# Rounded 512-column matmuls whose moving columns lie and are read in pieces of eight

## The chip, the cores and the metric

The kernel runs on one core of one Trainium2 chip. The metric is the device time of one execution in microseconds (us); lower is better.

## The reference

Linear attention with random features, followed by a layer norm and a two-layer FFN with a residual. There are 8 batches, 8 heads, 576 positions, 64 columns per head and 128 features; the model width is 512 and the FFN's inner width 2048. All data are float32.

```python
def phi(x):                                   # x: q or k, scaled by 64 ** -0.25
    h = x @ omega.T - sum(x * x) / 2
    return exp(h - max(h)) / sqrt(128)

kv  = einsum('bhsm,bhsd->bhmd', phi(k), v)
num = einsum('bhsm,bhmd->bhsd', phi(q), kv)
den = einsum('bhsm,bhm->bhs', phi(q), phi(k).sum(over s)) + 1e-6
x   = num / den                               # 4608 rows of 512 columns
xn  = (x - mean(x)) / sqrt(var(x) + 1e-6) * g_ln
out = x + relu(xn @ w_ch1) @ w_ch2
```

## The kernel before

One Python planner (`Plan`) writes the program. Pieces of work are generators that name the engine and an assumed cost for each step; the planner picks, step by step, which piece goes next on which engine, and so fixes each engine's instruction order before the program is built. The costs are constants in the code, so the order does not depend on what a step really takes on the chip.

The 4608 rows of x are cut into 9 blocks of 512 rows (index `t`), each of 4 chunks of 128 rows (`i`). Attention work for later blocks is woven between the FFN matmuls of earlier ones.

**Rounded matmuls.** The FFN matmuls work on float32 numbers split in two parts of type fp32r: a rounded copy, and the rest (the number minus the rounded copy, rounded again). A product of two such numbers takes three matmuls: high x high, low x high, high x low. `w[:, 0]`, `xnT[:, 0]` and `hl[:, 0]` are high parts, `[:, 1]` the low ones. Every such matmul has a stationary operand of 128 x 128 (loaded by an LDWEIGHTS of its own, PEld in the profile) and a moving operand of 128 x 512, and writes one PSUM bank of 512 columns.

- `mm1(t, f)` (lines 798 to 800): for each of the 16 slices `f` of the inner width, 4 steps over the model width by 3 matmuls. Stationary are columns of `w_ch1`, moving is `xnT` (the 512 rows of the block as columns). `relu` (lines 809, 811) turns the bank into `hl`.
- `mm2(t, f)` (lines 831 to 833): for each slice `f` and each chunk `i`, 3 matmuls. Stationary are 128 columns of `hl`, moving is a row block of `w_ch2`. Sums are kept in four banks over all `f`; `result` (line 842) adds x and stores.
- `gen_q2` (lines 589, 590): the projection of q for the later blocks, two rounded matmuls per 512 columns, with `qs` as the moving operand: `qs` holds the rounded q in partitions 0 to 63 and the rest of it in 64 to 127.

**Where the moving operands come from.** `xnT` is filled in `gen_xnT1` from four transposes in one PSUM bank: line 775 (ScalarE) copies and rounds, line 777 (VectorE) subtracts to get the rest. `xnT` has one buffer, so the block's four chunks are transposed between the last `mm1` of one block and the first of the next, under the last `mm2`. `w_ch2` comes as 64-bit numbers whose two words `gen_w` puts together on ScalarE and VectorE (lines 352 to 385), element by element, for the 16 slices of each weight once, mostly in the first 150 us. `qs` is loaded from `qD` and rounded in lines 580 and 582, element by element too.

**Other matmuls** that the text speaks of: line 308 is a bf16 matmul of 128 x 256 columns on constant data, which keeps TensorE busy before the first FFN matmul; lines 483, 514, 554 and 681 are attention matmuls on unrounded float32 with 64 rows or 64 columns of the array; line 771 holds the transposes.

In all, 6 x 576 FFN matmuls and 2 x 56 for q are rounded with 512 columns.

Of the kernel before, what the change touches and what calls it, by code (L numbers as in the profile page):

```python
# [17 lines left out]
ALU = mybir.AluOpType  # L18
# [4 lines left out]
P = 128  # L23
B, H, S, D = 8, 8, 576, 64
M = 128
DM = H * D
DFF = 4 * DM
NP = H // 2
NK = DM // P
NF = DFF // P  # L30
# [9 lines left out]
QB = 256  # L40
NB = N // QB
# [27 lines left out]
class Plan:  # L69
# [73 lines left out]
    def free(self, *names):  # L143
        for n in names:
            assert n not in self.places, n
            self.places[n] = self.cur.seen()
            self.cur.holds -= n[0] == "b" and 0 < self.cur.holds
            self.wake(lambda w: w[0] == "get" and n in w[1])

    def done(self, key):  # L150
        self.made[key] = self.cur.seen()
        self.wake(lambda w: w == ("wait", key))
# [38 lines left out]
def favor_ffn(ctx, tc, kT, kTr, vF, vR, qT, qD, omT, gT, w1, w2, out):  # L191
# [12 lines left out]
    nc = tc.nc  # L204
# [8 lines left out]
    def f32(ap):  # L213
        return ap.bitcast(F32)

    def act(n, k=1, c=0.09):
        return "run", {ACT: k * (c + 0.00084 * n)}

    def dve(n, k=1, c=0.065):
        return "run", {DVE: k * (c + 0.00105 * n)}  # L220

    def us(eng, t):
        return "run", {eng: t}

    def dma(n):
        return "run", {SP: n * 4e-6 / 0.36}
# [13 lines left out]
    def wait(*key):  # L240
        return "wait", key
# [4 lines left out]
    def tile_of(tag, shape, dtype=F32, pool=None):  # L246
        pool = pool or (wp if tag[1].isdigit() and tag[0] == "w" else small if tag[0:2] in ("kv", "mb", "st") or tag[0] == "v" else sb)
        return pool.tile(shape, dtype, tag=tag, name=tag, bufs=1)

    def heads_of(tag):  # L250

        n = H * (D + 1)
        return tile_of(tag, [P, -(-n // LINE) * LINE])[:, 0:n].rearrange("p (a b) -> p a b", b=D + 1)

    def bank(tag, n=512):
        return tile_of(tag, [P, 512], F32, ps)[:, 0:n]
# [12 lines left out]
    def at_now():  # L269
        return b_at if mlp_on else banks  # L270
# [22 lines left out]
    om_raw = tile_of("hid0", [P, M])  # L293
    if TILED:
        om = const.tile([P, M], F32, name="om")
        om_hi = const.tile([P, M], F32R, name="om_hi")
        om_lo = const.tile([P, M], F32R, name="om_lo")
# [12 lines left out]
    def gen_const():  # L310
        yield dma(P * M)
        nc.sync.dma_start(om_raw, omT)
        yield dve(M)
        if TILED:
            nc.vector.tensor_scalar(out=om, in0=om_raw, scalar1=SC, scalar2=None, op0=ALU.mult)
# [11 lines left out]
    def slot(h):  # L327
        return (h % 2) * 4 + h // 2 if TILED else h

# [62 lines left out]
    kvs, phis, xs, xnTs, pvs, pvt = {}, {}, {}, {}, {}, {}  # L392
# [30 lines left out]
    def gen_k(b, c, kraw, v, early, t_v, n_kp):  # L423
# [14 lines left out]
        def values():  # L438
            yield us(DVE, 0.08)
            nc.vector.memset(v[:, :, D : D + 1], 1.0)  # L440
            done(("v", b, c))
# [64 lines left out]
        plan.add(rank, values())  # L506
        if TILED:
            t_b = yield "get", at_now(), 2
# [28 lines left out]
    def gen_q(blk, j):  # L537
# [8 lines left out]

        if TILED:
            t_b = yield "get", at_now(), 2
# [20 lines left out]
    def gen_q2(blk, j, s):  # L569
        rank = plan.cur.rank  # L570
        q_turn = yield "get", turn["q"]
        t_q = yield "get", n_big
        qraw = tile_of(t_q, [P, 2 * QB])
        yield dma(P * 2 * QB)
        nc.sync.dma_start(qraw, qD[blk, j, s].rearrange("p a b -> p (a b)"))
        yield wait("om2")
        t_s = yield "get", n_big
        qs = tile_of(t_s, [P, 2 * QB], F32R)
        yield act(2 * QB)
        nc.scalar.copy(out=qs, in_=qraw)  # L580
        yield us(DVE, 0.85)
        nc.vector.tensor_tensor(out=qs[D:P], in0=qraw[D:P], in1=f32(qs[D:P]), op=ALU.subtract)  # L582
        free(t_q, q_turn)
        t_b = yield "get", at_now()

        plan.cur.after = max(plan.cur.after, plan.cur.end + LATE)
        yield us(PE, 0.46)
        pq = bank(t_b)
        nc.tensor.matmul(pq, om_hi, qs, start=True, stop=False)  # L589
        nc.tensor.matmul(pq, om_lo, qs, start=False, stop=True)  # L590
        free(t_s)
        yield from features(blk, j, s, t_b, pq)

# [7 lines left out]
    def features(blk, j, s, t_b, pq):  # L601
        t_c = yield "get", n_big
        qc = tile_of(t_c, [P, 2 * QB])
        eng = yield "run", {ACT: 0.48, DVE: 0.62} if blk >= T // QB else {ACT: 0.58}
        copy(eng, qc, pq)
        free(t_b)
        mx_turn = yield "get", turn["mx"]
        t_m = yield "get", n_big
        mx = tile_of(t_m, [P, 2 * QB])
        yield us(POOL, 1.9)  # L610
        nc.gpsimd.partition_all_reduce(mx, qc, P, bass_isa.ReduceOp.max)  # L611
        done(("mx", blk, j, s))
        yield us(DVE, 0.95 if blk >= T // QB else 0.6)
        nc.vector.tensor_tensor(out=qc, in0=qc, in1=mx, op=ALU.subtract)  # L614
        free(t_m, mx_turn)
        yield act(2 * QB)
        nc.scalar.activation(out=qc, in_=qc, func=AF.Exp)  # L617
        phis[blk, j, s] = t_c, qc.rearrange("p (a b) -> p a b", b=QB)
        done(("phi", blk, j, s))

    def phi(blk, h, cols):
        p, o = h // 2, h % 2
        s, i = (o, p % 2) if TILED else (p % 2, o)
        return phis[blk, p // 2, s][1][:, i, cols]
# [137 lines left out]
            plan.add(plan.cur.rank, gen_xnT1(t, i, xn, t_n, xn_turn))  # L762

    def gen_xnT1(t, i, xn, t_n, xn_turn):
        xnT = xnTs[t][1]
        yield wait("ident")
        t_b = yield "get", at_now()
        yield us(PE, 0.46)
        pt = bank(t_b).rearrange("p (a b) -> p a b", b=P)
        for k in range(NK):  # L770
            nc.tensor.transpose(pt[:, k], xn[:, k * P : (k + 1) * P], ident)  # L771
        free(t_n, xn_turn)
        cols = slice(i * P, (i + 1) * P)
        yield us(ACT, 0.5)
        nc.scalar.copy(out=xnT[:, 0, :, cols], in_=pt)
        yield dve(DM)
        nc.vector.tensor_tensor(out=xnT[:, 1, :, cols], in0=pt, in1=f32(xnT[:, 0, :, cols]), op=ALU.subtract)  # L777
        free(t_b)
        done(("xnT", t, i))


    hid = {}

    def mm1(t, f):
        for k in range(NK):
            yield wait("w", 1, f // NK * NK + k)
        for i in range(TC):
            yield wait("xnT", t, i)
        if not mlp_on:
            mlp_on.append(True)  # L790
        t_x, xnT = xnTs[t]
        t_b = yield "get", b_h
        ph = bank(t_b)
        for k in range(NK):
            yield us(PE, 3 * 0.225)
            w = wparts[1, f // NK * NK + k]
            cs = slice(f % NK * P, (f % NK + 1) * P)
            nc.tensor.matmul(ph, w[:, 0, cs], xnT[:, 0, k], start=(k == 0), stop=False)  # L798
            nc.tensor.matmul(ph, w[:, 1, cs], xnT[:, 0, k], start=False, stop=False)  # L799
            nc.tensor.matmul(ph, w[:, 0, cs], xnT[:, 1, k], start=False, stop=(k == NK - 1))  # L800
        if f == NF - 1:
            free(t_x)
        plan.add(MOST_URGENT, relu(t, f, t_b, ph))

    def relu(t, f, t_b, ph):
        t_h = yield "get", n_hid
        hl = tile_of(t_h, [P, 2, T], F32R)
        yield act(T, 1, 0.05)
        nc.scalar.activation(out=hl[:, 0], in_=ph, func=AF.Relu)  # L809
        yield dve(T)  # L810
        nc.vector.scalar_tensor_tensor(  # L811
            out=hl[:, 1], in0=ph, scalar=0.0, in1=f32(hl[:, 0]), op0=ALU.max, op1=ALU.subtract
        )
        free(t_b)
        hid[t, f] = t_h, hl
        done(("hid", t, f))

    accs = {}

    def mm2(t, f):  # L820
        yield wait("w", 2, f)
        yield wait("hid", t, f)
        t_h, hl = hid[t, f]
        w = wparts[2, f]
        for i in range(TC):
            if f == 0:
                t_b = yield "get", (b_acc[i],)
                accs[i] = bank(t_b)
            yield us(PE, 3 * 0.225)
            cs = slice(i * P, (i + 1) * P)  # L830
            nc.tensor.matmul(accs[i], hl[:, 0, cs], w[:, 0], start=(f == 0), stop=False)  # L831
            nc.tensor.matmul(accs[i], hl[:, 0, cs], w[:, 1], start=False, stop=False)  # L832
            nc.tensor.matmul(accs[i], hl[:, 1, cs], w[:, 0], start=False, stop=(f == NF - 1))  # L833
            if f == NF - 1:
                plan.add(MOST_URGENT, result(t, i, accs[i]))
        free(t_h)
# [55 lines left out]


TILED = True
LINE = 16
FIRST = 4
N_BIG = 14
# [4 lines left out]
WARM, COLD = 0.0, 5.0  # L902
RW, RS = -10, 1.0
RK, RQ = -36, -28


# [37 lines left out]
```

## Time and profile before

| | |
|---|---|
| median of 3 runs | 1012.5 us (1011.98 to 1012.75) |
| the profiled execution, its own time | 1012.24 us |
| its span from the first to the last instruction | 1010.4 us |
| TensorE busy | 1004.0 us (99%), 6794 matmuls |
| weight loads (PEld) busy | 813.7 us (81%) |
| VectorE busy | 499.9 us (49%) |
| ScalarE busy | 343.1 us (34%) |
| GpSimd busy | 137.1 us (14%) |
| mean granted TensorE clock | 0.999 |

The profile is of one execution. Its page lists, for each engine, the busy time, then groups of equal instructions: line of the program, engine, operation, output tile <- input tiles, shapes and count, and after the bar the busy us, the mean ns of one, and the idle time of the engine just before them with what ended it. A timeline row is: start in us, duration in us, engine, line, operation, and how many are merged into the row (x3). Matmuls are pipelined: the record of one reaches past the start of the next, so what a row of equal matmuls costs is read from their starts and not from their durations. PEld is TensorE's weight load, which runs beside the matmul before it.

### The profile page before, as it was taken

Reading aid. Unit: us, or ns where it says so; the run is one execution under the profiler, and the core shown is the slowest. Engines: PE = TensorE matmul, PEld = TensorE weight load, DVE = VectorE, ACT = ScalarE, POOL = GpSimd, SP = SyncE. Lnnn points to the kernel's source line nnn. Section 1 sums busy time; section 2 is a strip of 40 time slices with the busy share of each in tenths; the row PEclk is TensorE's granted clock in tenths of the full one; section 3 lists DMA queues with packets and bytes.
Section 4 is the critical chain, followed back from the end, with each engine's and each line's share of the span. In section 5 each row is a group of like instructions: output and inputs, shape, how many; then the busy total and the mean of one; then the engine's idle time right before and its main releaser. Section 6 shows DMA issues by size and latency. Waiting matters only on the chain.

```text
span 1010.4 us, 16487 instructions
## 1 busy us (share of the span) xinstructions
PE 1004.0 (99%) x6794; PEld 813.7 (81%) x6794; DVE 499.9 (49%) x1054; ACT 343.1 (34%) x785; POOL 137.1 (14%) x80
## 2 busy tenths in 40 slices
PE   9999999999999999999999999999999999999998
PEld 7877787787778778887888778888888888888886
DVE  6999997375347531673157423751384143113112
ACT  6687755235334520353125321331142011011110
POOL 5000632023001300140005000220031000000000
PEclk9999999999999999999999999999999999999999
DMA  9544332221132100320031100300120010001001
GB/s 353 205 145 162 121 105 73 75 74 64 43 116 76 41 12 1 128 84 1 1 126 64 43 1 11 116 1 1 42 84 1 1 42 1 0 1 42 1 1 42
DMA packets 29740, 63.16 MB, mean 63 GB/s; under 512 B 3424, under 2 KB 3552, under 8 KB 29664
## 3 DMA queue, kind: packets, MB, share of 16 engines
q1 hardware_dynamic: 29664, 62.09, 17.7%
q8 instruction: 54, 0.88, 0.3%
q14 instruction: 22, 0.18, 0.1%
HBM read 52.64 MB, written 9.44 MB: 61 GB/s over the span
## 4 chain that ended last, share of the span: by engine, by line
PE 94%; DVE 4%; DMA 1%; issue 0%; SPq 0%; ACT 0%; DVEq 0%
PE b L798 14%; PE b L831 14%; PE b L800 13%; PE b L799 13%; PE b L832 13%; PE b L833 13%; PE b L681 3%; PE b L514 3%; PE b L483 3%; PE b L771 1%; PE b L589 1%; PE b L590 1%; DMA w<-w 1%; DMA w<-vF 1%; PE b L554 0%; DVE x L842 0%
## 5 line engine op out<-in xcount | busy, mean ns | idle before, releaser
L811 DVE SCALAR_TENSOR_TENSOR hid<-b,hid 128x512 fp32r<-128x512 f32 x144 | 99.4, 690 | 381.2 <-ACT hid L809 381.0
L809 ACT ACTIVATE hid<-b 128x512 fp32r<-128x512 f32 x144 | 86.7, 602 | 457.2 <-PE b L800 456.5
L831 PE MATMUL b<-w,hid 128*128 128x512 f32 x576 | 232.0, 403 | 0.0
L798 PE MATMUL b<-xnT,w 128*128 128x512 f32 x576 | 230.2, 400 | 0.0
L833 PE MATMUL b<-w,hid 128*128 128x512 f32 x576 | 224.8, 390 | 0.0
L832 PE MATMUL b<-w,hid 128*128 128x512 f32 x576 | 224.8, 390 | 0.0
L800 PE MATMUL b<-xnT,w 128*128 128x512 f32 x576 | 224.6, 390 | 0.1
L799 PE MATMUL b<-xnT,w 128*128 128x512 f32 x576 | 224.6, 390 | 0.0
L611 POOL PARTITION_ALL_REDUCE wide<-wide x72 | 136.0, 1927 | 630.4 <-ACT wide L230 463.4
L798 PEld LDWEIGHTS b<-xnT,w 128*128 128x128 f32 x576 | 108.1, 188 | 25.6 <-issue 0.7
L831 PEld LDWEIGHTS b<-w,hid 128*128 128x128 f32 x576 | 108.1, 188 | 25.3 <-issue 0.7
L800 PEld LDWEIGHTS b<-xnT,w 128*128 128x128 f32 x576 | 108.1, 188 | 23.6 <-DVE xnT L777 0.5
L833 PEld LDWEIGHTS b<-w,hid 128*128 128x128 f32 x576 | 108.1, 188 | 23.2
L799 PEld LDWEIGHTS b<-xnT,w 128*128 128x128 f32 x576 | 108.2, 188 | 20.8
L832 PEld LDWEIGHTS b<-w,hid 128*128 128x128 f32 x576 | 108.3, 188 | 20.2
L451 ACT ACTIVATE kp<-b,mb 128x128 f32<-128x128 f32 x272 | 74.7, 388 | 60.9 <-DVE mb L445 60.7
L614 DVE TENSOR_TENSOR wide<-wide,wide 128x512 f32<-128x512 f32 x72 | 63.7, 890 | 10.0 <-POOL wide L611 9.4
L445 DVE TENSOR_REDUCE mb<-b 128x4 f32<-128x512 f32 x72 | 46.6, 683 | 35.5 <-PE b L514 35.5
L617 ACT ACTIVATE wide<-wide 128x512 f32<-128x512 f32 x72 | 45.3, 634 | 45.8 <-DVE wide L614 45.3
L681 PEld LDWEIGHTS b<-kv,wide 128*64 128x64 f32 (+1 forms) x1088 | 40.5, 140 | 11.4 <-issue 8.8
L582 DVE TENSOR_TENSOR wide<-wide,wide 64x512 fp32r<-64x512 f32 x56 | 43.7, 787 | 8.7 <-ACT wide L580 7.2
L230 ACT COPY wide<-b 128x512 f32<-128x512 f32 x60 | 34.1, 593 | 36.0 <-PE b L590 31.2
(70 smaller groups left out, 784.1 us busy)
## 6 DMA issues: line engine op xcount, KB each, us to landing
w<-w SPq DMA_DIRECT2D x32, 512.0 KB, 7.8
wide<-qD SPq DMA_DIRECT2D x56, 256.0 KB, 2.7
out<-x SPq DMA_DIRECT2D x36, 256.0 KB, 2.0
v<-vF SPq DMA_DIRECT2D x28, 260.0 KB, 3.1
wide<-kT SPq DMA_DIRECT2D x28, 256.0 KB, 3.1
wide<-qT SPq DMA_DIRECT2D x8, 256.0 KB, 3.9
w<-vF SPq DMA_DIRECT2D x4, 260.0 KB, 4.8
v<-vR SPq DMA_DIRECT2D x4, 260.0 KB, 4.0
```

Of the source, the lines that this page charges most:

```text
L451: nc.scalar.activation(out=kp[:, j], in_=pk[:, i], func=AF.Exp, scale=1.0, bias=mb[:, j : j + 1])
L611: nc.gpsimd.partition_all_reduce(mx, qc, P, bass_isa.ReduceOp.max)
L614: nc.vector.tensor_tensor(out=qc, in0=qc, in1=mx, op=ALU.subtract)
L681: nc.tensor.matmul(pn[a:z, i], phi(blk, h, slice(cols + a, cols + z)), kvs[b][1][:, h], start=True, stop=True)
L798: nc.tensor.matmul(ph, w[:, 0, cs], xnT[:, 0, k], start=(k == 0), stop=False)
L799: nc.tensor.matmul(ph, w[:, 1, cs], xnT[:, 0, k], start=False, stop=False)
L800: nc.tensor.matmul(ph, w[:, 0, cs], xnT[:, 1, k], start=False, stop=(k == NK - 1))
L809: nc.scalar.activation(out=hl[:, 0], in_=ph, func=AF.Relu)
L811: nc.vector.scalar_tensor_tensor(out=hl[:, 1], in0=ph, scalar=0.0, in1=f32(hl[:, 0]), op0=ALU.max, op1=ALU.subtract)
L831: nc.tensor.matmul(accs[i], hl[:, 0, cs], w[:, 0], start=(f == 0), stop=False)
L832: nc.tensor.matmul(accs[i], hl[:, 0, cs], w[:, 1], start=False, stop=False)
L833: nc.tensor.matmul(accs[i], hl[:, 1, cs], w[:, 0], start=False, stop=(f == NF - 1))
```

## The change

The 512 moving columns of a rounded matmul are taken as 4 groups of 16 pieces of 8 columns: column `c * 128 + a * 8 + b` with `c` below 4, `a` below 16, `b` below 8. Before, column n lay at element n of its row. Now it lies at element `a * 32 + c * 8 + b`. A matmul reads its columns in the old logical order, so that it takes the first eight elements of each 32 across the row, then the second eight, and so on: four passes over 2048 bytes. Its output columns are written in order, side by side, as before. Everything that fills a moving operand puts it into the new layout: `xnT` by the copies out of PSUM, where chunk `i` is group `c`; `w_ch2` and `qD` by the host, which reorders the arrays before the launch (`spread`). Stationary operands (`w_ch1`, `hl`, `om_hi`, `om_lo`) lie as before. `rounded` stands for the 8 former matmul calls; its line number is 786 in the changed kernel. The planner's costs and ranks stay, and the order of the instructions on every engine is the same as before.

```diff
+    def rounded(out, lhsT, rhs, start, stop):
+        nc.tensor.matmul(
+            out.rearrange("p (c a b) -> p c a b", a=AW, b=BW), lhsT,
+            rhs.rearrange("p (a c b) -> p c a b", a=AW, b=BW), start=start, stop=stop,
+        )
...
 def gen_q2(blk, j, s):
-        nc.sync.dma_start(qraw, qD[blk, j, s].rearrange("p a b -> p (a b)"))
+        nc.sync.dma_start(qraw, qD[blk, j, s])
...
-        nc.tensor.matmul(pq, om_hi, qs, start=True, stop=False)
-        nc.tensor.matmul(pq, om_lo, qs, start=False, stop=True)
+        rounded(pq, om_hi, qs, start=True, stop=False)
+        rounded(pq, om_lo, qs, start=False, stop=True)
...
 def gen_xnT1(t, i, xn, t_n, xn_turn):
-        xnT = xnTs[t][1]
+        xnT = xnTs[t][1].rearrange("p h k (a c b) -> p h k a c b", a=AW, b=BW)[:, :, :, :, i]
...
-        cols = slice(i * P, (i + 1) * P)
+        pt = pt.rearrange("p k (a b) -> p k a b", b=BW)
-        nc.scalar.copy(out=xnT[:, 0, :, cols], in_=pt)
+        nc.scalar.copy(out=xnT[:, 0], in_=pt)
-        nc.vector.tensor_tensor(out=xnT[:, 1, :, cols], in0=pt, in1=f32(xnT[:, 0, :, cols]), op=ALU.subtract)
+        nc.vector.tensor_tensor(out=xnT[:, 1], in0=pt, in1=f32(xnT[:, 0]), op=ALU.subtract)
...
 def mm1(t, f):
-            nc.tensor.matmul(ph, w[:, 0, cs], xnT[:, 0, k], start=(k == 0), stop=False)
-            nc.tensor.matmul(ph, w[:, 1, cs], xnT[:, 0, k], start=False, stop=False)
-            nc.tensor.matmul(ph, w[:, 0, cs], xnT[:, 1, k], start=False, stop=(k == NK - 1))
+            rounded(ph, w[:, 0, cs], xnT[:, 0, k], start=(k == 0), stop=False)
+            rounded(ph, w[:, 1, cs], xnT[:, 0, k], start=False, stop=False)
+            rounded(ph, w[:, 0, cs], xnT[:, 1, k], start=False, stop=(k == NK - 1))
...
 def mm2(t, f):                                # the three calls likewise, on accs[i], hl and w
+AW, BW = 16, 8
+def spread(x):
+    x = x.reshape(*x.shape[:-1], -1, AW, BW)
+    return np.ascontiguousarray(np.moveaxis(x, -3, -2)).reshape(*x.shape[:-3], -1)
...
-    qD = np.ascontiguousarray(np.concatenate([q6, q6], axis=3))
+    qD = spread(np.concatenate([q6, q6], axis=3).reshape(NB, 2, 2, P, 2 * QB))
-    w2 = np.ascontiguousarray(moe_w_ch2.reshape(NF, P, DM)).view(np.int64)
+    w2 = spread(moe_w_ch2.reshape(NF, P, DM)).view(np.int64)
```

More of the change, by code (lines that the diff above doesn't have):

```diff
@@ L830, in mm2 @@
             cs = slice(i * P, (i + 1) * P)
-            nc.tensor.matmul(accs[i], hl[:, 0, cs], w[:, 0], start=(f == 0), stop=False)
-            nc.tensor.matmul(accs[i], hl[:, 0, cs], w[:, 1], start=False, stop=False)
-            nc.tensor.matmul(accs[i], hl[:, 1, cs], w[:, 0], start=False, stop=(f == NF - 1))
+            rounded(accs[i], hl[:, 0, cs], w[:, 0], start=(f == 0), stop=False)
+            rounded(accs[i], hl[:, 0, cs], w[:, 1], start=False, stop=False)
+            rounded(accs[i], hl[:, 1, cs], w[:, 0], start=False, stop=(f == NF - 1))
             if f == NF - 1:
```

## The prediction

> **What bounds the kernel now.** I read the page's first part and its clock line, then the chain, then the groups, then single matmuls in time order.
>
> ```profile
> PE 1004.0 (99%) x6794; PEld 813.7 (81%) x6794; DVE 499.9 (49%) x1054; ACT 343.1 (34%) x785; POOL 137.1 (14%) x80
> ...
> PEclk9999999999999999999999999999999999999999
> ...
> PE 94%; DVE 4%; DMA 1%; issue 0%; SPq 0%; ACT 0%; DVEq 0%
> PE b L798 14%; PE b L831 14%; PE b L800 13%; PE b L799 13%; PE b L832 13%; PE b L833 13%; PE b L681 3%; PE b L514 3%; PE b L483 3%; PE b L771 1%; PE b L589 1%; PE b L590 1%; DMA w<-w 1%; DMA w<-vF 1%; PE b L554 0%; DVE x L842 0%
> ```
>
> TensorE is busy for 99% of the span at the full granted clock, and the chain lies on it for 94%. Six lines, 798 to 800 and 831 to 833, hold about 80% of the span. They are the three-part products of the two FFN matmuls; with lines 589 and 590 they are exactly the matmuls that the change touches.
>
> ```profile
> L831 PE MATMUL b<-w,hid 128*128 128x512 f32 x576 | 232.0, 403 | 0.0
> L798 PE MATMUL b<-xnT,w 128*128 128x512 f32 x576 | 230.2, 400 | 0.0
> L833 PE MATMUL b<-w,hid 128*128 128x512 f32 x576 | 224.8, 390 | 0.0
> L832 PE MATMUL b<-w,hid 128*128 128x512 f32 x576 | 224.8, 390 | 0.0
> L800 PE MATMUL b<-xnT,w 128*128 128x512 f32 x576 | 224.6, 390 | 0.1
> L799 PE MATMUL b<-xnT,w 128*128 128x512 f32 x576 | 224.6, 390 | 0.0
> ...
> L589 PE MATMUL b<-wide,om_hi 128*128 128x512 f32 x56 | 21.8, 389 | 0.0
> L590 PE MATMUL b<-wide,om_lo 128*128 128x512 f32 x56 | 21.8, 389 | 0.0
> ```
>
> That is 6 x 576 + 2 x 56 = 3568 rounded matmuls, and TensorE sat idle before none of them for more than 0.1 us in sum. The 390 ns of a record is not what one costs, since they overlap; that is the step from one start to the next. A long quiet stretch near the end gives it (timeline; first and last of 182 rounded matmuls in a row):
>
> ```profile
> 959.83 0.39 PE L832 MATMUL b<-w,hid 128*128 128x512 f32 x1
> ...
> 1000.86 0.39 PE L800 MATMUL b<-xnT,w 128*128 128x512 f32 x1
> ```
>
> 41.03 us over 181 steps is 226.7 ns each. 3568 x 226.7 ns = 809 us: one price, paid 3568 times, is four fifths of the kernel. So the question is only what the new way of reading the moving columns does to this step.
>
> **What the step is made of.** The nearest other matmul at full clock with a weight load before each is the bf16 warming matmul of 256 columns, 36 of them in a row:
>
> ```profile
> 38.07 0.27 PE L308 MATMUL b<-spin 128*128 128x256 bf16 x1
> ...
> 38.58 4.09 PE L308 MATMUL b<-spin 128*128 128x256 bf16 x36
> ```
>
> (4.09 - 0.27) / 35 = 109.1 ns for 256 columns, 218.3 ns for 512, though that holds two starts. The rounded step is 8.4 ns longer for the same columns. Is that a fixed fee of a rounded matmul, or a stall that comes from how its data are read? Right after a switch to the small attention matmuls and back, the same instructions with the same shapes run like this (first and last of eight in a row):
>
> ```profile
> 363.10 0.40 PE L832 MATMUL b<-w,hid 128*128 128x512 f32 x1
> ...
> 364.74 0.39 PE L833 MATMUL b<-w,hid 128*128 128x512 f32 x1
> ```
>
> 1.64 us over 7 steps is 234.3 ns. After some ten matmuls it settles at 226.7 again, and nothing waits in between. A fixed fee cannot do that. What differs is how the load of the next weights lies against the moving stream; in the settled state it starts with the matmul that it runs under:
>
> ```profile
> 900.20 0.39 PE L799 MATMUL b<-xnT,w 128*128 128x512 f32 x1
> 900.20 0.19 PEld L800 LDWEIGHTS b<-xnT,w 128*128 128x128 f32 x1
> ```
>
> So I read the 8.4 ns, and the further 7.6 ns of the disturbed ones, as two read streams getting in each other's way in SBUF: the load walks 512 bytes of its row in order, the moving stream 2048 bytes. A stall that depends on where two streams meet is one that another order of addresses can change, either way.
>
> **The change, part by part.** No instruction is added, removed or moved: each engine's order is the same, the transfers have the same sizes and rows, and the host lays `w2` and `qD` out anew before the launch. Three things cost or save.
>
> First, the 3568 rounded matmuls read eight columns (32 bytes), skip 24, and so on, in four passes. Their results still land side by side in PSUM. No row of this trace has a moving operand with gaps, so the new step is bounded by the nearest rows: 218.3 ns below (the bf16 pair) and 234.3 ns above (the disturbed matmuls), that is -8.4 to +7.6 ns, -30.0 to +27.1 us. I take the lower one. In each pass the moving stream now keeps to one 32-byte place in every 128 bytes, while the load passes that place a quarter of the time, and in whole pieces; if meetings cause the stall, most of them should go, and the bf16 pair is the row with the lightest load stream. This is the choice on which the forecast stands, and it is argued, not seen.
>
> Second, the whole saving cannot be had where another engine is at its limit too:
>
> ```profile
> 50.00:150.00 100.00, 99.93 (x711) 78.29 (x709) 98.62 (x193) 72.78 (x151) 24.20 (x12) 1.00 0.38 134
> ```
>
> From 50 to 150 us (columns: length, then busy us of PE, PEld, DVE, ACT, POOL) VectorE is busy for 98.62 of 100 us, splitting the weights. A faster TensorE would wait for it. In that stretch lie these:
>
> ```profile
> L798 PE MATMUL b<-xnT,w 128*128 128x512 f32 x58 | 23.6, 407 | 0.0
> ...
> L831 PE MATMUL b<-w,hid 128*128 128x512 f32 x52 | 21.3, 410 | 0.0
> ```
>
> With their two sister lines each that is 3 x 58 + 3 x 52 = 330, whose 330 x 8.4 ns = 2.8 us I count as lost to VectorE. Where the rounded step gets longer, nothing is lost there, and the loads, casts and subtractions are hidden as before.
>
> Third, the 36 copies (line 775, ScalarE) and 36 subtractions (777, VectorE) that fill `xnT` now write pieces of eight, and 777 also reads them.
>
> ```profile
> L777 DVE TENSOR_TENSOR xnT<-b,xnT 128x512 fp32r<-128x512 f32 x36 | 23.9, 685 | 6.7 <-ACT xnT L775 6.6
> L368 DVE SCALAR_TENSOR_TENSOR wide<-w 128x512 uint32<-128x512 uint32 x32 | 22.7, 724 | 0.0
> L775 ACT CAST xnT<-b 128x512 fp32r<-128x512 f32 x36 | 20.5, 588 | 21.8 <-PE b L771 21.7
> L352 ACT ACTIVATE wide<-w 128x512 uint32<-128x512 uint32 x24 | 15.7, 682 | 0.0
> ```
>
> Lines 368 and 352 touch every other word, a rougher access than runs of eight, and take 724 and 682 ns. So the price lies between nothing and 39 + 94 = 133 ns for a pair, and I take nothing. At a block's change the cover is this:
>
> ```profile
> 918.23 0.68 DVE L777 TENSOR_TENSOR xnT<-b,xnT 128x512 fp32r<-128x512 f32 x1
> ...
> 919.49 0.39 PE L798 MATMUL b<-xnT,w 128*128 128x512 f32 x1
> ```
>
> The last subtraction ends at 918.91, 0.58 us before the first matmul that needs it: 133 ns fit in. With the cover gone (the first block, whose last subtraction TensorE waits for) it is 0.1 us once.
>
> Sum: 1012.24 (the profiled execution, 0.26 below the median of 1012.5) - 30.0 + 2.8 + 0 = 985.0 us.
>
> The Trainium skill, "TensorE: Matmul & The Clock Gate", section "Back-to-back issue gap", gives N / 2.4 + 2.5 ns, so 215.8 ns for 512 columns. By it the saving would be up to 10.9 ns a matmul and the sum, with the same loss to VectorE, an estimated 977 us. The rounded matmuls of this trace do not keep to that figure: they step by 226.7 ns.
>
> **The rivals.** (1) Nothing happens: the settled 8.4 ns are a fee for four-byte columns whatever their addresses, and only the disturbed part hangs on the load. For it: in all quiet stretches the step is the same, for two different lines and all tiles. Against it: the disturbed steps. Time: 1012. The Trainium skill, "SBUF — State Buffer", section "Who interferes with whom", says that TensorE has two independent read ports, one for the moving operand and one for the weights, so that loads cost the stream nothing; by that rule, too, no order of addresses could win here. The trace agrees in so far as the load hides under the matmul, and not in that the step goes from 226.7 to 234.3 ns with nothing else changed.
>
> (2) Slower: the stream pays for each jump. If the 8.4 ns are what the reader pays for going from one stretch of a row to the next, then a row of 64 pieces has more such places than one that runs through. Break-even with the gain above is 8.4 / 64 = 0.13 ns a piece; at twice that the step is 8.4 ns longer, 3568 x 8.4 = 30 us, and the time 1042 us. For it: a run is cut every 32 bytes, and no row here shows jumps for free. Against it: both strided rows above pay little for worse jumps, though on other engines.
>
> (3) More meetings, not fewer: the disturbed state becomes the settled one, 1012.24 + 27.1 = 1039 us. For it: what the present order settles at is among the lowest steps in the trace. Against it: in a pass the two streams share one place in four.
>
> **How the numbers follow.** Saving, 0.57: 985, own range 968 to 1003. Its low end lets a third more go than the bf16 pair shows, since that pair holds two starts (1012.24 - 40 = 972), and a little for the disturbed steps; its high end leaves two thirds of the stall. Nothing, 0.18: 1012. Jumps, 0.15, and more meetings, 0.10, spread from 1015 to over 1050 around their prices. Faster by more than 0.2% (2 us, about what a measurement of this kernel can tell from no change): 0.57; within 0.2%: 0.18; slower: 0.25. The range 968 to 1035 holds the first two and the smaller third of the slower ones, and leaves out under 2 in 10.
>
> **What would show it.** Right: in the quiet stretch near 960 us the step is about 218 ns, VectorE stays near 98% from 50 to 150 us with TensorE now waiting there, and lines 775 and 777 stay below 690 and 730 ns. Wrong: a step of 226.7 ns and about 1012 us (a fee), or of 235 ns and more (jumps or meetings). If the step falls and the time does not, TensorE has idle time before lines 798 and 831 that names VectorE.

## The result, and the profile after

The changed kernel takes 1005.31 us (median of 4 runs, 1004.26 to 1005.58) against 1012.62 us for the kernel before on the same chip: a ratio of 0.9925, 95% interval 0.9907 to 0.9942. That is 7.3 us less. The forecast was 27 us less. The profiled execution has a span of 1002.5 us, 7.9 us under the span of before.

From the page of the changed kernel: busy times, the chain, the rounded matmuls (one line now for all, 786), and the two operations that fill `xnT` (from the answer by lines; columns as before).

```profile
PE 994.9 (99%) x6794; PEld 814.1 (81%) x6794; DVE 500.5 (50%) x1054; ACT 342.4 (34%) x785; POOL 136.7 (14%) x80
...
PE 88%; DVE 8%; issue 1%; DMA 1%; ACT 1%; SPq 0%; DVEq 0%; ACTq 0%
...
L786 PE MATMUL b<-w,hid 128*128 128x512 f32 x1728 | 430.1, 391 | 0.0
L786 PE MATMUL b<-xnT,w 128*128 128x512 f32 x1728 | 426.6, 390 | 0.1
...
L777 DVE TENSOR_TENSOR xnT<-b,xnT 128x512 fp32r<-128x512 f32 x36 | 23.9, 686 | 6.6 <-ACT xnT L775 6.6
L775 ACT CAST xnT<-b 128x512 fp32r<-128x512 f32 x36 | 20.5, 587 | 21.6 <-PE b L771 21.6
```

TensorE is busy 9.1 us less (994.9 for 1004.0) and idle 1.2 us more: that is the whole difference of the spans. The record of a rounded matmul is 390 or 391 ns (390 to 403 before), so the groups again say nothing about the step. The copy and the subtraction cost what they cost before (587 and 686 ns).

The step is read from the chain, which now joins successive rounded matmuls because they share a line (start, length, line, count; all pieces over 20 us):

```profile
372.61 29.26 PE b L786 x126
472.15 36.51 PE b L786 x165
590.45 29.26 PE b L786 x126
656.56 62.01 PE b L786 x268
755.43 62.02 PE b L786 x268
836.33 71.48 PE b L786 x324
911.61 85.16 PE b L786 x387
```

Length over count is 232, 221, 232, 231, 231, 221 and 220 ns. These are the same matmuls on the same kind of data, and there are two prices. From start to start, in the trace, the cheap stretches step by 219 and 221 ns in turn, 220.0 on the mean; the dear ones repeat five steps, 237, 227, 229, 230, 230 (a nanosecond more or less), 230.7 on the mean. Hardly anything lies between: of 2576 steps in stretches of 20 steps and more, 1379 lie in stretches that end at 220.0, 1156 in stretches that end at 230.7, and 41 in one that does neither. Before the change all 34 of these stretches end at 226.7 or within half a nanosecond of it.

Over all 3443 pairs of rounded matmuls in a row, in 125 stretches, the mean step went from 231.59 (before) to 228.85 ns, and 3443 x 2.74 ns = 9.4 us. Half of that is no matter of the settled price: 4.8 us lie in the first eleven steps of the stretches. The very first step, behind other matmuls, is about 330 ns in both kernels; in the ten behind it the kernel before comes down to 226.7 only slowly (233.6 ns on the mean in the first five of them, in the 34 long stretches), while the changed one is near its price at once (227.2). The other 4.6 us lie in the 2321 steps behind these eleven.

The windows show it against the kernel before: 50 us each, TensorE's busy time, the matmuls that touch the window, the granted clock, the DMA's share and GB/s, first of before, then of after.

```profile
760.00:810.00 50.00, 50.00 (x222) 1.00 0.00 1
...
930.00:980.00 50.00, 50.00 (x222) 1.00 0.00 1
```

```profile
760.00:810.00 50.00, 50.00 (x219) 1.00 0.00 1
...
930.00:980.00 50.00, 50.00 (x229) 1.00 0.00 1
```

At 930 us the changed kernel does 229 matmuls where the old one did 222; at 760 us it does fewer than the old one. The granted clock is 1.00 in all four windows and the DMA's share 0.00, so neither of them makes the difference. So the question became what makes one stretch cheap and the next dear.

### The profile page after: what moved, and what is told of

It reads as the page before. It is cut to its first block, busy times and chain, and to the rows that moved or that the text cites. A ratio compares the mean times of both kernels' runs of the same rounds, so it can differ in the third digit from the quotient of the medians.

```text
span 1002.5 us, 16490 instructions
## 1 busy us (share of the span) xinstructions
PE 994.9 (99%) x6794; PEld 814.1 (81%) x6794; DVE 500.5 (50%) x1054; ACT 342.4 (34%) x785; POOL 136.7 (14%) x80
## 4 chain that ended last, share of the span: by engine, by line
PE 88%; DVE 8%; issue 1%; DMA 1%; ACT 1%; SPq 0%; DVEq 0%; ACTq 0%
PE b L786 77%; PE b L681 3%; PE b L514 3%; PE b L483 3%; PE b L771 2%; DVE wide L368 1%; DVE w L354 1%; DVE w L379 1%; DVE mb L445 1%; DMA w<-w 1%; DVE hid L818 1%; DVE wide L614 1%; DMA w<-vF 1%; DVE w L385 0%; DVE x L849 0%
## 5 line engine op out<-in xcount | busy, mean ns | idle before, releaser
L786 PE MATMUL b<-w,hid 128*128 128x512 f32 x1728 | 430.1, 391 | 0.0
L786 PE MATMUL b<-xnT,w 128*128 128x512 f32 x1728 | 426.6, 390 | 0.1
L681 PE MATMUL b<-kv,wide 128*64 128x65 f32 (+1 forms) x1088 | 45.1, 227 | 0.0
L483 PEld LDWEIGHTS b<-v,kp 128*64 128x64 f32 (+2 forms) x1120 | 34.0, 138 | 13.5 <-issue 9.5
L483 PE MATMUL b<-v,kp 128*64 128x65 f32 (+2 forms) x1120 | 39.5, 226 | 0.7 <-DVE xnT L777 0.7
L514 PEld LDWEIGHTS b<-om,wide 64*128 64x128 f32 x512 | 31.1, 187 | 11.2 <-issue 7.8
L499 DVE TENSOR_TENSOR kv<-b,kv 128x260 f32<-128x260 f32 x56 | 23.2, 425 | 30.3 <-PE b L483 29.6
L514 PE MATMUL b<-om,wide 64*128 64x128 f32 x512 | 37.2, 285 | 0.0
L580 ACT CAST wide<-wide 128x512 fp32r<-128x512 f32 x56 | 33.4, 624 | 0.0
L696 DVE TENSOR_TENSOR x<-b,st 128x256 f32<-128x256 f32 x72 | 28.5, 418 | 0.4
```

The lines of the kernel that those rows point to most:

```text
L483: nc.tensor.matmul(pv[s, n][m, i], kp[r, slot(h), m], v[r, h], start=(n > 0 or c + i == 0), stop=(n > 0 or (c == NFULL and i == 3)),)
L514: nc.tensor.matmul(pk[h][:, p], kraw[a, p], om[a], start=True, stop=True)
L681: nc.tensor.matmul(pn[a:z, i], phi(blk, h, slice(cols + a, cols + z)), kvs[b][1][:, h], start=True, stop=True)
L786: nc.tensor.matmul(out.rearrange("p (c a b) -> p c a b", a=AW, b=BW), lhsT, rhs.rearrange("p (a c b) -> p c a b", a=AW, b=BW), start=start ...
```

## The experiments

Programs m1 to m6 hold only rounded matmuls of 128 x 128 by 512 on constant data, with a few other matmuls between; they leave out the whole computation, and their total time means nothing. "Settled" below is the mean step from start to start once it repeats. In a row of the timeline it is the length less one record (0.39 us), over the count less one. Programs r1 to r8 are the whole kernel. Code that is left out is marked with three dots.

**The moving pattern by itself.** m1 sets each of 13 patterns five times in a row of 40, entered by three kinds of other matmuls.

```diff
+    return t.rearrange("p (a c b) -> p c a b", c=period // piece, b=piece), period // piece
...
+        dst = big if c == 1 else big.rearrange("p (c a b) -> p c a b", c=c, b=piece)
...
+            for _ in range(REPEAT):                                     # REPEAT = 40
+                nc.tensor.matmul(dst, stat(sts[st]), src, start=True, stop=True)
```

> Leaves out the whole computation: 40 rounded matmuls in a row of the same shapes (128x128 stationary, read in order; 128x512 moving), for 13 ways of reading the moving row (pieces of 2 to 64 elements, one of each 4 or each 2 of such pieces and so on), each entered five times after a stretch of other matmuls. Theory 1 (two read streams meet): the row read as a whole settles at 226.7 ns as in the kernel before; pieces of 8 of 32 settle at 220.0 or in the cycle of five steps with mean 230.7, depending on the entry; other pieces have values of their own that do not order by the number of pieces. Theory 2 (a price per jump): steps rise with the number of pieces, 64 ns-free pieces of 8 lie at 220 only by chance, 2 of 8 (256 pieces) is the slowest, 64 of 256 (8 pieces) is at 226 to 227. Theory 3 (a fee): all at 226.7.

Timeline of m1, from one settled stretch each (start, length, tile, count): the whole row, 2 of 8, 4 of 16 from two entries, 8 of 32, 16 of 64, 32 of 128.

```profile
14.81 6.51 PE L89 MATMUL big<-whole,st 128*128 128x512 f32 x28
...
69.74 13.56 PE L89 MATMUL big<-twoEight,st 128*128 128x512 f32 x29
...
166.70 7.09 PE L89 MATMUL big<-fourSixteen,st 128*128 128x512 f32 x31
177.84 6.29 PE L89 MATMUL big<-fourSixteen,st 128*128 128x512 f32 x27
...
229.62 6.62 PE L89 MATMUL big<-eightThirtytwo,st 128*128 128x512 f32 x28
...
273.64 6.63 PE L89 MATMUL big<-sixteenSixtyfour,st 128*128 128x512 f32 x27
...
328.82 6.46 PE L89 MATMUL big<-thirtytwoOneTwentyeight,st 128*128 128x512 f32 x27
```

By these rows the settled steps are 226.7 ns (whole), 461 (2 of 8, whose record is 0.64 us), 223.3 and 226.9 (4 of 16: from one entry and from four), 230.7 (8 of 32, from all five entries), 240.0 (16 of 64; 239.5 over its cycle of 13 steps) and 233.5 (32 of 128; 233.3 over more steps). A price per jump is out: 128 pieces of four cost less than 32 pieces of sixteen. A fixed fee is out too. And 8 of 32 never came to 220.0 here, which the kernel shows in half of its stretches. The seven patterns that are not shown lie between 226.7 (64 of 256) and 259 ns, and three of them have two prices each, by entry: 231.1 or 233.3 (4 of 8), 232.4 or 233.3 (8 of 16), 233.3 or 259 (8 of 64). So two prices are no peculiarity of 8 of 32.

**The stationary operand's addresses.** m2 leaves the way of reading the moving operand as it was and changes where the 128 weights lie. Each case has tiles of its own, so the tiles' base addresses differ as well.

```diff
+    ("wholeA", (512, 512), "stA", at(0)),            # at(o): columns o to o + 127
+    ("wholeB", (512, 512), "stB", at(8)),
...
+    ("wholeH", (512, 512), "stH", at(0, 96)),        # 96 columns
...
+    ("eightB", (8, 32), "stB", at(8)),
...
+    ("eightE", (8, 32), "stE", every(4, 0)),         # every fourth column
```

> Leaves out the whole computation: the same matmuls, with the moving row read as a whole or in pieces of 8 of 32, against nine ways in which the 128 stationary columns lie (in order from element 0, 8 or 16; every 4th element, every 32nd element from 0, 8, 16 or 24; 96 columns only). Theory 1 (two streams meet): the step changes with the stationary operand alone. With every 32nd element the load stays in one 32-byte place of each 128; if places are what meets, the moving stream in pieces of 8 of 32 goes without a stall (216 to 218 ns) where the load keeps to place 2 or 3, which the stream reads only after the load is done, and not where it keeps to place 0 or 1. 96 columns shorten the stall by about a quarter (223 to 224 ns with the whole row). Theory 2 and 3 (jump or fee of the moving operand): the step does not depend on the stationary operand: 226.7 for the whole row with all of them.

Timeline of m2: the whole row with the weights in order, 8 columns on, and only 96 of them; then 8 of 32 with the weights 8 columns on, and with every fourth.

```profile
14.62 6.74 PE L105 MATMUL big<-wholeA,stA 128*128 128x512 f32 x29
...
68.69 5.53 PE L105 MATMUL big<-wholeB,stB 128*128 128x512 f32 x23
...
393.75 6.60 PE L105 MATMUL big<-wholeH,stH 128*96 128x512 f32 x28
...
500.67 6.51 PE L105 MATMUL big<-eightB,stB 128*128 128x512 f32 x28
...
607.79 6.59 PE L105 MATMUL big<-eightE,stE 128*128 128x512 f32 x27
```

226.8, 233.6, 230.0, 226.7 and 238.5 ns (the last without a short cycle: 237 to 240 by entry). The moving row of the first three is read alike. Between the first two only the place of the weights in their tile and the tiles' bases differ, and the bases by themselves seem not to matter: with the weights in order the whole row gives 226.7 in m1 and in m6, in other tiles, and in the kernel before, in many. The record of the load is 188 ns in both. So the step depends on where the weights lie, as it should if two read streams meet, which the prediction supposed; the meeting itself is in no record. The shape that I had given to it failed twice: a load of a quarter fewer columns (161 ns for 188) makes the step longer (230.0 for 226.8, where I had expected about three quarters of the stall), and weights that keep to another 32-byte place than the moving columns do not make it free (233.3 to 241 ns). The cases with every fourth and every 32nd column test two things at once, since there the load itself takes 303 to 315 ns.

**Offsets.** m3 moves either operand by 2 to 32 columns.

> Leaves out the whole computation: rounded matmuls in a row again, with the stationary columns or the moving row started some elements later. If only the distance between the two streams' addresses counts, a moving row started 8 elements later gives what a stationary row started 8 elements earlier or later gave (226.6 ns for pieces of 8, 233.3 for the whole row), and a start 32 elements later gives again what element 0 gives (230.7 and 220.0; 226.7). If the absolute place of the stationary operand counts, the moving operand's start changes nothing. Settled steps are multiples of 6.67 ns over a cycle of a few matmuls (220.0, 226.7, 233.3, or means of such cycles), whatever the offset. I look for a pair that settles at 220.0 or less from every entry.

With 8 of 32 the settled step is 229.2 or 236.7 ns with the weights 2 columns on, 236.7 or 233.3 with 4, 230.0 with 6, 220.0, 226.7 or 233.3 by entry with 12, 233.3 with 24 and 229.5 with 32. Eight columns on for the moving operand give 230.0, and eight for the weights 226.7 (m2): where each lies counts, not only how far apart. Weights 32 columns on do not give again what column 0 gives, as I had expected. The whole row, too, can settle at two prices: with the weights 4 columns on it came to 226.7 from three entries and to 233.4 from two. No rule that I tried gives these numbers.

**The entry.** m4 comes into the same 8-of-32 stretch through different matmuls.

```diff
+        for j in range(0, 32, 2):
+            thin(160)                                    # a bf16 matmul of 160 columns
+            thin(160 + j)
+            for _ in range(28 if mv == "eight" else 16):
+                one_of(mv, piece, period)
...
+    for kick in kicks:                                   # eight kinds of other matmuls
+        for _ in range(7):
+            kick()
+            for _ in range(20):
+                one_of("eight", 8, 32)
```

> Leaves out the whole computation: runs of rounded matmuls entered from two bf16 matmuls whose length grows by 2 columns (0.83 ns) from run to run, 16 times, for pieces of 8, the whole row and pieces of 4; then 20 matmuls in pieces of 8 after each of eight kinds of interruption, seven times each. Theory phase lock: with pieces of 8 the lock (220.0, or the cycle with mean 230.7) changes with the length of the entry, both occur, and the same entry from the same lock gives the same lock; the whole row reaches 226.7 from all. Theory data or place: all 16 runs of one pattern settle alike. An interruption that ends in 220.0 at least 6 times of 7 would be a way to choose the lock.

Timeline of m4: the settled part after two bf16 matmuls, and after one.

```profile
18.69 4.78 PE L67 MATMUL big<-eight,st 128*128 128x512 f32 x21
...
407.12 2.70 PE L67 MATMUL big<-eight,st 128*128 128x512 f32 x11
```

219.5 and 231.0 ns by these rows (220.0 and 230.7 over ten settled steps): same instruction, same addresses, both prices in one program. The length of the entry did not matter as I had expected (220.0 for all 16 values of j); one other matmul in between brought 230.7, seven times of seven, and eight pairs of 64-row matmuls brought 220.0, seven of seven. Of these seven only the first came from 230.7; the others found 220.0 already. m5 tried 13 entries and m6 seven more:

> Leaves out the whole computation: each time one matmul over the whole row (after it pieces of 8 have always settled at 230.7 ns), 16 matmuls in pieces of 8, one of 13 ways to disturb them, and 18 more. Theory phase lock: without a disturbance all stay at 230.7; the disturbances that end far from where they began in the load's course end at 220.0, and do so all four times, as the state before them is the same; two bf16 matmuls of 160 columns do (from the good lock they have kept it 16 times of 16), row pairs do, one bf16 matmul does not. If the lock were chosen by chance, each way would end half and half. Half and quarter matmuls (256, 128 of the columns) are open: either lock.

> Leaves out the whole computation. First part: as in the run on ways in, with shorter ways: 1, 2 or 4 pairs of row-tiled matmuls (8 pairs ended at 220.0 six times of six), 1, 2 or 4 transposes, and 16 half-column matmuls. Theory phase lock: one of the shorter ways ends at 220.0 six times of six whatever the state before (4 pairs the likeliest); by chance it would be half. Second part: 15 ways of reading the row by 5 starts of the moving operand (0, 4, 8, 16, 32 elements later) by three entries, 26 matmuls each. Pieces under 16 bytes aside, every settled step is 219.9 to 260 ns and the mean over a cycle; none is under 219.9, since 220.0 has been the lowest lock of all. Pieces of 8 in many short visits (8 of 128, 8 of 256) show whether the number of passes matters: by a price per jump they equal 8 of 32.

In m5 eight pairs of 64-row matmuls gave 220.0 six times of six, three other entries gave 230.7 each time, and nine gave now one, now the other. One of the three is two bf16 matmuls of 160 columns. Behind such a pair m4 had 220.0 sixteen times, but there the stretch ahead was at 220.0 already, all but the first time; here it was at 230.7. So the state before counts with the entry. In m6 four pairs of 64-row matmuls gave 220.0 six times of six; one transpose gave it three times of six, two gave it six of six, four gave it two of six. Its search over 15 patterns and 5 places of the moving operand found no settled step under 220.0 ns. Timeline of m6, two transposes between 8-of-32 matmuls:

```profile
190.40 1.08 PE L69 MATMUL big<-eight,st 128*128 128x512 f32 x4
191.31 0.38 PE L89 MATMUL sc<-ident,one 128*128 128x128 f32 x2
191.45 4.23 PE L69 MATMUL big<-eight,st 128*128 128x512 f32 x18
```

The 18 matmuls behind take (4.23 - 0.39) / 17 = 226 ns with the first long step, and 220.0 once settled. I read this as a way to choose the beat. It was too few different cases: the first four of the six all stood at the same place of the five-step cycle (behind a 230 that follows a 229), and the last two came from 220.0 already.

**Other pieces in the kernel.** r1 takes pieces of 4 of 16, r2 of 16 of 64, r3 leaves `xnT` and `qs` in order and only the second FFN matmul in pieces.

```diff
-AW, BW = 16, 8
+AW, BW = 32, 4        # r1;  r2: AW, BW = 8, 16
```

> The changed kernel with pieces of 4 of each 16 (128 pieces a row). By the settled steps of the matmuls run by themselves (223.35 ns from one entry, 226.8 to 226.95 from four), 3568 x 0 to 3.3 ns less than before: 1001 to 1013 us, likeliest 1009. By a price per jump it would be slower than pieces of 8: over 1020 us.

> The changed kernel with pieces of 16 of each 64 (32 pieces a row). By the settled steps of the matmuls run by themselves (239.2 to 239.95 ns), 3568 x 13 ns more than before: 1050 to 1060 us. By a price per jump it would lie between before and pieces of 8: 1005 to 1013 us.

> The kernel before with pieces of 8 in the second FFN matmul alone (lines 831 to 833); the first one and q read whole rows. If each matmul had its own price, half of what the change gains: 1012.6 - 3.7 = 1009 us. Theory phase lock: every 12 matmuls the way of reading changes, and each change throws the streams out of their lock; a matmul over the whole row has always been followed by the lock at 230.7, and its own way back to 226.7 takes some eight matmuls at a mean of 231 to 233. So a mean step of 230 to 231 ns, 3 to 4 ns more than before: 1021 to 1027 us.

r1 1006.12 us (ratio 0.9937, 0.9915 to 0.996), r2 1052.18 us (1.0388, 1.0358 to 1.0418), r3 1016.39 us (1.0036, 1.0021 to 1.0051). The last three long pieces of the chain of r1, the last two of r2, then one group of the second FFN matmul from the timeline of r3:

```profile
754.44 60.06 PE b L786 x268
833.43 73.63 PE b L786 x324
910.84 87.73 PE b L786 x387
```

```profile
870.32 77.78 PE b L786 x324
951.99 94.84 PE b L786 x396
```

```profile
950.24 2.93 PE L786 MATMUL b<-w,hid 128*128 128x512 f32 x12
```

224, 227 and 227 ns in r1, 240 in r2, as m1 had shown for these patterns. So the small program carries over, two prices with it. r1 is about as fast as pieces of 8 although most of its stretches settle near the 226.7 of before: of its 7.1 us in the steps, 5.3 lie in the first eleven of the stretches. r3 was slower, as the theory of the beat said, but by less (I had expected 1021 to 1027 us): its whole-row groups fell back to 226.7 ns at once, and only the pieces stayed near 231 ((2.93 - 0.39) / 11).

**Transposes in the kernel.** r4 puts two transposes into ten stretches, r5 into 23, and r6 is the changed kernel again.

```diff
 def mm1(t, f):
         for k in range(NK):
             yield us(PE, 3 * 0.225)
+            if k == 0 and (t, f) in TURNS:
+                for i in range(2):
+                    nc.tensor.transpose(ph[:, i * P : (i + 1) * P], ident, ident)
```

> The changed kernel with two transposes of the identity (128 x 128) put in at ten places of the FFN, each inside a long stretch of rounded matmuls that ran at 230.7 ns a step; they write into a PSUM bank that the next matmul starts anew, and nothing else moves. Theory (the stretch keeps the beat that it was started in, and two transposes start the beat of 220.0 ns): about 750 matmuls go from 230.7 to 220.0 ns, 8.0 us gained, and ten times 0.26 us spent, so about 1000 us (998 to 1003), and the long stretches near 660, 755 and 590 us show 220.0 ns. Rival (the beat hangs on where the operands lie in SBUF or on what the other engines do at that time, and not on how the stretch was started): the steps stay at 230.7 ns and the time is 1007 to 1009 us.

> The same with 23 places, the shorter stretches (20 to 40 matmuls) too. Theory: some 330 matmuls more gain 10.7 ns each, 3.5 us, and 13 places more cost 0.26 us each, 3.4 us, so 998 to 1004 us, no different from ten places. Rival: 1010 to 1012 us.

> The changed kernel again, unaltered, on the same chip as the two with transposes. Theory: 1004 to 1006.5 us, and the same stretches at 230.7 and at 220.0 ns as in its first profile, since what stands ahead of a stretch is the same. Rival (the beat is drawn anew in each execution): the total is alike but the stretches near 660 and 755 us are at 220.0 in some and those near 840 and 910 at 230.7.

r4 1007.32 us, r5 1003.7 us, r6 1005.47 us (ratios to before 0.9944, 0.9912 and 0.9928, the intervals about 0.0014 to either side). The chain's two dear long stretches, in r6, r4 and r5:

```profile
657.22 62.02 PE b L786 x268
756.09 62.02 PE b L786 x268
```

```profile
662.05 59.72 PE b L786 x259
761.11 59.74 PE b L786 x259
```

```profile
661.95 57.02 PE b L786 x259
758.91 57.02 PE b L786 x259
```

r6 repeats the first profile from 211 us on: every stretch of 20 matmuls and more holds the same step as there, so the price of these is not drawn anew in each run. Before that the two differ: the 78 matmuls from 50 us on, where VectorE is near its limit, settled at 220.0 in the first profile and at 230.7 in r6. In r4 the transposes did not help: still 230.6 ns a matmul (59.72 / 259), and the time is the rival's. In r5 both stretches run at 220.2 ns (57.02 / 259). The second was at 220.0 already when its transposes came; in the first the same two transposes at the same place brought it over from 230.7, and r5 differs ahead of them only by more transposes. So neither the addresses nor the place in the program, with what the other engines do there, fix the price of a stretch. In the trace the steps just ahead of the transposes differ: where r5 went over at 662 us, the last step between rounded matmuls was the long one (... 230, 230, 237), and where r4 stayed it was another. Over r4 and r5, four of five entries behind the long step went over, and none of those at another place of the cycle; a stretch at 220.0 stayed at 220.0 every time.

**The place in the cycle.** r7 and r8 test that: two transposes in each of the four long dear stretches, in r7 behind the long step, in r8 elsewhere.

```diff
+TURNS = {(2, 12), (4, 12), (5, 6), (6, 10)}    # r7;  r8: {(2, 13), (4, 14), (5, 8), (6, 6)}
```

> The changed kernel with two transposes of the identity at four places, one in each of the four long stretches that run at 230.7 ns, put where the step just before the last rounded matmul is the long one of the five (…230, 230, 237, then the transposes). Theory (the beat after the transposes follows from the place in the five-step cycle at which they come; in the runs with ten and 23 places, four of five entries at this place of the cycle went over to 220.0 ns, and none of eleven entries at another): the remaining 86, 86, 230 and 134 matmuls go to 220.0 ns, 536 x 10.7 ns = 5.7 us less 4 x 0.25 us, so about 1000.7 us (999.5 to 1002). Rival (chance, or the other transposes that stood ahead of those places): the stretches stay at 230.7 ns and the time is 1006 to 1007 us.

> The same four stretches, two transposes each, but one or two matmul groups earlier or later, where the step before is another of the five (230 after 230, or 230 after 229). Theory of the place in the cycle: all four stretches stay at 230.7 ns and the time is 1005.4 + 4 x 0.25 = 1006.4 us (1005.5 to 1007.5). Rival (it is the place in the program, not in the cycle): at least one of them goes over, as in the other kernel.

r7 1000.89 us (ratio 0.9885, 0.9871 to 0.9898), r8 1003.73 us (0.9911, 0.9898 to 0.9925). The chain's pieces behind the transposes, r7 and then r8:

```profile
382.82 19.18 PE b L786 x87
...
600.00 19.18 PE b L786 x87
664.99 50.86 PE b L786 x231
...
783.82 29.74 PE b L786 x135
```

```profile
389.36 13.88 PE b L786 x63
...
612.53 8.97 PE b L786 x39
...
678.38 42.20 PE b L786 x183
...
766.37 50.84 PE b L786 x231
```

r7: 220 ns in all four, and the time within 0.2 us of what the theory gave. r8: 220 ns in the first and the last, 230 and 231 in the two between. I had expected all four to stay, so that half failed, and by what was put down before the run it is the rival's outcome. But the two that went over both stood behind a 230 that follows a 230, the two that stayed both behind a 230 that follows a 229. This reading was made after the run. The traces of r4, r5, r7 and r8 together bear it out. Of the entries from a stretch at 230.7, those behind the long step went over to 220.0 in 8 cases of 9 and those behind the last 230 in 2 of 2. Those behind the 227, behind the 229 and behind the 230 that follows it did so in none of 8, 3 and 3. So in this kernel the place in the cycle decides in 24 entries of 25, and the list of good places is longer than I had thought. It is not the whole rule: in m6 two transposes behind a 230 that follows a 229 went over four times of four, and in r8 they stayed; those of m6 read other tiles. r7 is the best version here, 4.6 us under r6 and the only one under 1003 us.

## Why the prediction was partly right

**The bound: right. The mechanism: right in kind.** TensorE set the end, and the price of a rounded matmul is a stall that depends on addresses and on the entry, not a fee and not a price per jump (m1, m2). That two reads in SBUF meet fits this and is not shown; what they would share stays open. The Trainium skill, "SBUF — State Buffer", section "Who interferes with whom", has TensorE's two read ports independent; for these matmuls m2 does not fit that, since a move of the weights by 32 bytes took the step from 226.8 to 233.6 ns while their load kept its 188 ns.

**The first term of the sum: the step that failed.** It put -8.4 ns on all 3568 rounded matmuls, -30.0 us, taking the bf16 pair's 218.3 ns. Measured: 220.0 ns, -6.7, in somewhat over half of the steps of the long stretches, and 230.7 ns, +4.0, in most of the rest; with the shorter stretches and the first steps -2.7 ns on the mean, 9.4 us. The cheap state was foreseen within 2 ns (near 960 us, where the prediction looked, it is 220.0; that it looked into a cheap stretch is luck). That a stretch could settle at a dearer step as well was not in the sum, which gave one settled step to all 3568 matmuls: it stood there only as rival (3), for all stretches at once and at 234.3 ns. In the kernel before, every long stretch came down to 226.7; in pieces of eight a dear state can settle and last through 267 steps. So rival (3), which had a chance of 0.10, came true in 1156 of 2576 long steps, at about half its price. The first steps of a stretch, which the prediction let into the low end of its range as "a little for the disturbed steps", are half of what was gained (4.8 us of 9.4). The argument by 32-byte places, from which the choice of the lower bound came, does not fit m3: weights 32 columns on keep the same places, and the step is 229.5 ns instead of 220.0 or 230.7.

**VectorE's term: right in kind, small.** From 50 to 150 us:

```profile
50.00:150.00 100.00, 99.23 (x713) 78.94 (x712) 98.75 (x192) 72.47 (x151) 23.57 (x12) 1.00 0.38 133
```

VectorE stays at 98.75 of 100 us, TensorE's idle time goes from 0.07 to 0.77 us (0.27 in the profile of r6), and VectorE's share of the chain doubles to 8%. So at most 0.7 us shows where 2.8 were put down; there was less to lose.

**The copies into `xnT`: right.** 587 and 686 ns against 588 and 685; taken as nothing.

## What to carry to other kernels

A step read from one quiet stretch is the price of a state, not of an instruction: before it is multiplied by thousands, look whether every stretch of the kernel has it, and whether a disturbed state always ends there. Where a new access order is priced by an old one's settled step, put the other settled steps of the trace into the range as mixtures, not only as rivals that hold everywhere. Price the steps of getting settled apart from the settled ones: here they were half of the gain. And a cure that works six times of six in a small program has been tried once if all six come in at the same moment.

## What the runs showed of the hardware

- Rounded 512-column matmuls settle at one step (220.0, 226.7, 233.3 or 240.0 ns, 6.7 apart) or at a cycle of steps with a mean of its own (223.3 over four, 230.7 over five, 239.5 over 13). The step depends on where both operands lie: 226.8 to 233.6 ns with the weights moved by 32 bytes (m2), 230.0 for 8 of 32 with the moving row moved by 32 bytes (m3).
- The same stream can hold two beats, 220.0 and 230.7 ns, through hundreds of matmuls; which one follows from the moment of entry and from the state before. r6 repeated the first profile stretch by stretch from 211 us on, and r7 chose the cheap one in four places of four for 0.25 us each. Little is needed to change it: in the changed kernel's first profile, near 148 us, one step of 234 for 220 ns, at a projection matmul of `gen_q2`, took a stretch from 220.0 to 230.7.
- One piece in four: moving columns in pieces of 8 bytes (2 of 8) cost 461 ns, in pieces of 16 bytes (4 of 16) 223 to 227, and wider pieces are not better (about 240 with 64 bytes of each 256). Wider gaps cost as well: 16 bytes of each 128 take 246.7 (m1), of each 256 some 277 (m6).
- Open: what the two streams share. No model of places that I tried gives the offsets of m3, and in m6 four transposes behind the same visible steps led once to 220.0 and once to 230.7, so something finer than a nanosecond's reading of the steps counts too. Why two of the five places of the cycle let the transposes bring the cheap beat and three do not, and why m6 differs at one of them, is not known.
